# Dealing weight conversions out over the first ups, and moving two checks and a load

## The chip, the cores and the metric

The kernel runs on one core of a Trainium2 chip. The metric is the device time of one execution, in microseconds. A run is compared with runs of the kernel before on the same chip.

A core has five engines with an instruction queue each, which they work through in order: TensorE (PE, matrix products; PEld are its weight loads), VectorE (DVE), ScalarE (ACT), GpSimd (POOL) and SyncE (SP), which here only issues DMAs. Engines wait for each other by semaphores.

## The reference

Two blocks in a row. The first is a gated linear recurrence over 768 steps for 4 batches of 8 heads, with 48 values a head. The second is a dense block over the 3072 tokens, with an activation that is a softmax times its input, and a normalisation:

```python
# q, k, v, alpha: (4, 8, 768, 48), single precision
for t in range(S):
    state = alpha[:, :, t, :, None] * state + np.einsum('bhd,bhe->bhde', k[:, :, t], v[:, :, t])
    y[:, :, t] = np.einsum('bhd,bhde->bhe', q[:, :, t], state)
x = y.transpose(0, 2, 1, 3).reshape(3072, 384)

h = x @ w_in                       # 384 -> 1024
e = np.exp(h - h.max(-1))
solu = h * e / (e.sum(-1) + 1e-09)
ln = (solu - mean(solu)) / np.sqrt(var(solu) + 1e-06) * g_ln
out = ln @ w_out                   # 1024 -> 384
```

`w_in` and `w_out` come in double precision; everything else, the output too, is single precision.

## The kernel before

**Groups.** The sequence is cut into six groups of 128 steps. A group takes that stretch of all four batches at once, so 512 tokens. Each group has an attention part (transposes, running products of alpha, masked scores, the products with the values, the state) and a dense part. The dense part has eight *ups* (`up_mm`, `up_act`), each for 128 of the 1024 inner features and all 512 tokens, and then eight half *downs*, four blocks of 128 tokens with two halves of the features.

**An up** is six matmuls on PE into a bank `h` of PSUM (tag "h", two banks), then on ACT the exponential `e` (L408), on DVE the product `room` = h·e (L409), and on ACT its square `u2` (L412). Up f+2 can start on PE only when `room` of up f has been formed, since that frees the bank. A callback given to `up_act` is put between L409 and L412. In the first group `e` and `u2` lie in four places that are used in turn; PE sums them over features with `array_sums`, once after up 3 and once after up 7.

**Order of the work.** Nothing is reordered: `manual_schedule` keeps each engine's instructions in the order in which the program gives them. So the order in the source is the order in each queue.

**The weights** are fetched in eight pieces (0 to 3 of `w_in`, 4 to 7 of `w_out`) as raw double words into `room`, six slots of 1536 words. Piece 0 goes to slot 3, piece 1 to slot 4, pieces 2 and 3 interleaved to slots 1 and 2, piece 4 to slot 3 again, 5 and 6 to 1 and 2, 7 to 3. A fetch into a slot waits until all that read the slot before have ended. In the first group the products of the ups go to the slots 0, 5 and 4, slot 4 from up 6 on.

Each piece is *converted* on DVE by `bits`, in five instructions over 128 x 768 words: L612, L615 (the upper word's bits moved and its sign put in), L620, L623, L624 (the lower word added). The intermediate values lie in `lots`, a pair for even and a pair for odd pieces. Pieces of `w_out` are then scaled by the gains on ACT (`scaled`, L631).

Each piece is also *checked* on ACT by `in_range`, with a square (L598) and an exponential (L601), each followed by the reading of its sum; the two halves can be issued apart. `alpha_over` is a check of a group's alpha of the same kind (L196, two instructions with two readings). The sums decide at the very end whether a second, general path runs; in these runs it doesn't.

**The first group's ups.** Before them pieces 0 and 1 are converted and checked. Before the change, `bits` of the pieces 2 to 5 is split between the ups, two steps behind an even up and three behind an odd one; pieces 6 and 7 are converted whole behind the last up. The halves of the checks of the pieces 2, 3 and 4 lie in the ups 0 to 5. The pieces 5 to 7 are checked later, in the second group.

**Behind the ups**, in the order of the source: `turned` for the keys of the second group (L164), `load` of the third group's keys, `array_sums`, `down(0, 0)`, `token_sums(0)` (on PE L462, on DVE L467 and three small instructions), `alpha_T(1)` (transposes on DVE, L179 and L182), `down(1, 0)`, `turned` for the queries, then on DVE the scans (L204) and products of the second group, the query products last (L799). On PE stand between them `mean` (L645, L652; it needs all of `w_out`) and more downs. Then PE does the scores of the second group (`scores(1, 0)`, L278); their banks are those from which L799 reads. The rows of the queries that the scores of the state need are moved by DMA (`move_lasts`, `move_firsts`), the state is decayed on GpSimd (`decay`, L261), and PE reads it (`read_state`, L333).

Of the kernel before, what the change touches and what calls it, by code (L numbers as in the profile page):

```python
# [11 lines left out]
U32 = mybir.dt.uint32  # L12
I32 = mybir.dt.int32
AF = mybir.ActivationFunctionType
ALU = mybir.AluOpType
# [17 lines left out]
def fast_path(ctx, tc, q, k, v, alpha, moe_w_in, moe_w_out, moe_g_ln, out):  # L33
# [65 lines left out]
    an = const.tile([P, H, TQ, D], FP, name="an")  # L99
# [31 lines left out]
    def load(src, dst, g):  # L131
        t = slice(g * P, (g + 1) * P)
        for b in range(B):
            nc.sync.dma_start(
                out=dst[32 * b : 32 * b + 32].rearrange("t h u d -> t h (u d)"),
                in_=src[b, :, t, :].rearrange("h (t u) d -> t h (u d)", u=TQ),
            )
# [5 lines left out]
    def load_first(src, dst, g):  # L143
        t = slice(g * P, (g + 1) * P)
        for b in range(0, B, 2):
            nc.sync.dma_start(
                out=by_token(dst)[:, b : b + 2].rearrange("p b h d -> p (b h) d"),
                in_=src[b : b + 2, :, t].rearrange("b h p d -> p (b h) d"),
            )
# [28 lines left out]
    def firsts(src, dst):  # L178
        nc.vector.transpose(out=dst.rearrange("p h (t u) -> p h u t", u=TQ), in_=src[:, :, :, 0:E0])  # L179

    def lasts(src, dst):
        nc.vector.transpose(  # L182
            out=dst.rearrange("p j (i t u) -> p u j i t", u=TQ, i=2),
            in_=src[:, :, :, E0:D].rearrange("p (j i) u d -> p u j i d", i=2),
        )

    def alpha_T(g):
        nc.gpsimd.memset(aT[:, :, 0:1], 0.0)
        firsts(an, aT[:, 0:H, 1:SW])
        lasts(an, aT[:, H:NB, 1:SW])  # L190

    def alpha_over(g):
        x = an.rearrange("p h u d -> p (h u d)")
        sq = one.tile([P, 768], FP, name="sq").bitcast(U8)[:, 0 : x.shape[1]]
        for i, sign in enumerate((1.0, -1.0)):
            nc.scalar.activation(  # L196
                out=sq, in_=x, func=AF.Relu, scale=sign, bias=mone, accum_out=over[:, g, i : i + 1]
            )
# [184 lines left out]
    def u_of(g, f):  # L383
        return slots[((0, 5, 4), (1, 2, 3))[g % 2][f // 3]][:, T4 * (f % 3) : T4 * (f % 3) + T4]
# [5 lines left out]
    def up_mm(g, f):  # L390
        d = gr[g]
        h = ps_h.tile([P, T4], FP, tag="h", name="h")
        for a in range(KC):
            nc.tensor.matmul(  # L394
                h, lhsT=w_in[:, a, f * P : (f + 1) * P], rhs=d["x"][:, a].rearrange("p b t -> p (b t)"),
                start=(a == 0), stop=(a == KC - 1),
            )
        d["h"] = h

    def up_act(g, f, between=None):  # L400
        d = gr[g]
        h = d["h"]
        if g:
            e, u2 = (ring.tile([P, T4], FP, name=x) for x in ("e", "u2"))
        else:
            e, u2 = (sT[:, f % 4, 4 * i : 4 * i + 4].rearrange("p b t -> p (b t)") for i in range(2))
        u = u_of(g, f)
        nc.scalar.activation(out=e, in_=h, func=AF.Exp)  # L408
        nc.vector.tensor_tensor(out=u, in0=h, in1=e, op=ALU.mult)  # L409
        if between:  # L410
            between()
        nc.scalar.activation(out=u2, in_=u, func=AF.Square)  # L412
        d[f] = e, u2
# [16 lines left out]
    def array_sums(g, half):  # L430


        d = gr[g]
        if half == 0:
            d["q"] = [ps_a.tile([P, T4], FP, tag=f"a{i}", name=f"quarters{i}") for i in range(2)]
        for i in range(2):
            for f in range(4):
                r = quarter(f)
                nc.tensor.matmul(
                    d["q"][i][r], lhsT=ones[:, 0:32], rhs=d[4 * half + f][i], start=half == 0, stop=half == 1,  # L440
                    tile_position=(0, r.start), skip_group_check=True,
                )
        if half:
            d["p"] = one.tile([P, 2, T4], FP, name="p")
            for i in range(2):
                nc.scalar.copy(out=d["p"][:, i], in_=d["q"][i])
            d["unit"] = small_ones
# [53 lines left out]
    def down(n, half, part=range(HF)):  # L501
        g, b = divmod(n, B)
        d = st[n]
        if half == 0 and 0 in part:
            d["o"] = ps_o.tile([P, 512], FP, tag="o", name="o")
        for f in (half * HF + i for i in part):
            nc.tensor.matmul(  # L507
                d["o"][:, 0 : DM + 1], lhsT=u_of(g, f)[:, b * P : b * P + P], rhs=w_out[:, f], start=(f == 0),
                stop=(f == FC - 1), skip_group_check=True,
            )  # L510
# [45 lines left out]
    float64 = moe_w_in.dtype != FP  # L556
# [4 lines left out]
    def place(i):  # L561
        kind, f = pieces[i]
        return w_out[:, f : f + 2, 0:DM] if kind else w_in[:, :, f * P : f * P + 2 * P]
# [22 lines left out]
    made = {}  # L586
# [3 lines left out]
    def in_range(i, parts=(0, 1)):  # L590


        if not float64:
            return
        if 0 in parts:
            hi = raws[i][:, :, :, 1].bitcast(FP)
            squares[i] = one.tile([P, F], FP, name="sq").rearrange("p (c f) -> p c f", c=hi.shape[1])
            nc.scalar.activation(out=squares[i], in_=hi, func=AF.Square, accum_out=far[:, i, 0:1])  # L598
        if 1 in parts:
            sq = squares.pop(i)  # L600
            nc.scalar.activation(out=sq, in_=sq, func=AF.Exp, scale=-(2.0**24), accum_out=far[:, i, 1:2])  # L601

    def bits(i, part=None):
        if not float64:
            return
        lo, hi = raws[i][:, :, :, 0], raws[i][:, :, :, 1]
        if part != 1:
            made[i] = [
                lots[2 * (i % 2) + x].rearrange("p (c f) -> p c f", c=hi.shape[1]) for x in range(2)
            ]  # L610
            top = made[i][0].bitcast(U32)
            nc.vector.tensor_scalar(  # L612
                out=top, in0=hi, scalar1=3, scalar2=0x3FFFFFF8, op0=ALU.logical_shift_left, op1=ALU.bitwise_and
            )
            nc.vector.scalar_tensor_tensor(  # L615
                out=top, in0=hi, scalar=0xC0000000, in1=top, op0=ALU.bitwise_and, op1=ALU.bitwise_or
            )
        if part != 0:
            top, low = made.pop(i)
            nc.vector.tensor_scalar(  # L620
                out=low.bitcast(U32), in0=top.bitcast(U32), scalar1=0xFF800000, scalar2=None, op0=ALU.bitwise_and
            )
            nc.vector.scalar_tensor_tensor(out=low, in0=lo, scalar=2.0**-52, in1=low, op0=ALU.mult, op1=ALU.mult)  # L623
            nc.vector.tensor_tensor(out=place(i), in0=low, in1=top, op=ALU.add)  # L624

    def scaled(i):
# [62 lines left out]
    def three(name, where):  # L689
        return [pool.tile([P, NP, P], FP, tag=tag, name=f"{name}{i}") for i, (pool, tag) in enumerate(where)]  # L690
# [13 lines left out]
    for i in range(3):  # L704
        part = slice(NP * i, NP * i + NP)
# [5 lines left out]
    for i in (0, 2, 1):  # L711
        if i == 1:
            scan_on(0, i)
        part = slice(NP * i, NP * i + NP)
        nc.vector.tensor_tensor(
            out=qe[:, :, 0:P] if i == 2 else qv[:, part, 0:P], in0=t[i], in1=aT[:, part, 1:SW], op=ALU.mult
# [13 lines left out]
    keys_back(0)  # L730
    in_range(0)
    bits(1)
    in_range(1)

    for f in range(FC):
        up_mm(0, f)
        if f == 4:
            array_sums(0, 0)
        up_act(0, f, (lambda: in_range(2 + f // 2, (f % 2,))) if f < 6 else None)

        bits(2 + f // 2, f % 2)
        if f == 0:
            next_state(0)
            fetch(4, 3)
            load_first(k, kn, 1)
            load_first(q, qn, 1)
            load(alpha, an, 1)
        elif f == 2:
            ends_k = ends_of(kn, "e")
        elif f == 3:  # L750
            fetch(5, 1)
            fetch(6, 2)
            ends_q = ends_of(qn, "u2")
        elif f == 5:
            fetch(7, 3)
            load_v(1)
        elif f == 6:
            scaled(4)
    bits(6)
    tk = three("tp_k", [(ps_a, "a2"), (ps_a, "a3"), (ps_h, "h")])  # L760
    turned(kn, ends_k, tk)
    load(k, kn, 2)
# [1 line left out]
    scaled(5)  # L764
    down(0, 0)
    scaled(6)
    bits(7)
    token_sums(0)
    alpha_T(1)
    down(1, 0)  # L770
    scaled(7)
    tq = three("tp_q", [(ps_a, "a0"), (ps_a, "a1")])
    turned(qn, ends_q, tq, range(H))
    for i in range(3):
        scan_back(1, i)
        part = slice(NP * i, NP * i + NP)
# [4 lines left out]
    mean(1)  # L781
    down(0, 1, (2, 3))
    hold(0)
    alpha_over(1)
    load(alpha, an, 2)
    tq += three("tp_q2", [(ps_h, "h")])
    turned(qn, ends_q, tq, range(H, NB))
    down(1, 1)
# [7 lines left out]
    for i in range(2):  # L796
        scan_on(1, i)
        part = slice(NP * i, NP * i + NP)
# [165 lines left out]
    def compare(out, x, bound, op):  # L964
# [6 lines left out]
        out=chunks[:, :, 2], in0=sums[:, :, 2], scalar=0.25, in1=sums[:, :, 3], op0=ALU.mult, op1=ALU.is_le  # L971
# [6 lines left out]
    else:  # L978
# [9 lines left out]
        out=bad, in0=all_ok[0:1, 0:1], scalar1=float(P * ends[-1]), scalar2=None, op0=ALU.is_lt  # L988
# [451 lines left out]
```

## Time and profile before

| | |
|---|---|
| median of 3 runs | 373.24 us (372.33 to 374.39) |
| the profiled execution | 374.51 us, of which the span in the profile is 372.6 us |
| mean granted TensorE clock | 0.995 |
| PE busy | 361.1 us, 97% of the span |
| DVE busy | 244.9 us, 66% |
| ACT busy | 147.2 us, 40% |
| POOL busy | 124.6 us, 33% |
| the first group's ups on PE | 28.8 to 53.3 us |
| the second group's ups on PE | from 101.6 us |

Times in the views are microseconds from the start of the span. In a timeline each line has the start, the length, the engine, the line of the kernel, the operation and its tiles; instructions of one kind in a row are merged (x48 stands for 48 of them). In square brackets stands how long the engine was idle before, and what it waited for. A line of windows has the stretch and its length, the busy time and number of instructions of PE, PEld, DVE, ACT and POOL, then PE's granted clock (1.00 is full speed), the share of the DMA engines, and GB/s. Matmuls are pipelined and their ends modelled, so PE's pace is best read from start to start.

### The profile page before, as it was taken

To read this page: it belongs to the slowest core of one execution; us is meant where nothing else is said; L and a number is where in the kernel's file an instruction comes from. 1 tells how busy PE (TensorE), PEld (TensorE's weight loads), DVE (VectorE), ACT (ScalarE), POOL (GpSimd) and SP (SyncE) were. 2 spreads that over 40 slices of the span, in tenths; PEclk is the share of its full clock that TensorE was granted. 3 is DMA by queue.
4 is the path that set the end of the run, shared out by engine and by line. 5 is a ranking of instruction groups with operands and counts; after the bars stand their busy time and mean duration, and the time that the engine had idled before them with its cause. 6 is when DMAs were issued, how large, how long until landed. Compare 5 with 4: busy or idle time off the path is not lost. (4 is left out here: it accounts for less than half of the span.)

```text
span 372.6 us, 10040 instructions
## 1 busy us (share of the span) xinstructions
PE 361.1 (97%) x4341; PEld 215.8 (58%) x4341; DVE 244.9 (66%) x375; ACT 147.2 (40%) x260; POOL 124.6 (33%) x129
## 2 busy tenths in 40 slices
PE   8889999979999999999999999999999999999994
PEld 7775355556755566566575566575555565555552
DVE  1997979978998888945666945666946223544500
ACT  3649853591556262251532251532231231332100
POOL 7020000001367973573114573114582211333200
PEclk9999999998999999999999999999999999999999
DMA  9995986066177608453036253004050000000011
GB/s 181 187 326 144 217 270 139 2 135 152 67 161 165 153 3 168 111 137 84 25 86 145 68 136 86 25 4 106 21 129 9 23 23 0 24 22 21 30 39 49
DMA packets 72871, 36.06 MB, mean 97 GB/s; under 512 B 48232, under 2 KB 70000, under 8 KB 72816
## 3 DMA queue, kind: packets, MB, share of 16 engines
q1 hardware_dynamic: 71792, 34.39, 39.5%
q10 hardware_dynamic: 1024, 0.92, 0.7%
q8 instruction: 36, 0.59, 0.7%
q14 instruction: 19, 0.16, 0.1%
HBM read 25.30 MB, written 4.72 MB: 81 GB/s over the span
## 5 line engine op out<-in xcount | busy, mean ns | idle before, releaser
L507 PE MATMUL o<-w_out,room 128*128 128x385 f32 x384 | 134.8, 495 | 0.0
L394 PE MATMUL h<-x,w_in 128*128 128x512 f32 x288 | 132.2, 599 | 0.6 <-ACT x L363 0.6
L507 PEld LDWEIGHTS o<-w_out,room 128*128 128x128 f32 x384 | 71.6, 191 | 55.3 <-issue 14.7
L394 PEld LDWEIGHTS h<-x,w_in 128*128 128x128 f32 x288 | 52.7, 189 | 58.3 <-issue 48.4
L409 DVE TENSOR_TENSOR room<-h,e 128x512 f32<-128x512 f32 x40 | 27.6, 690 | 60.0 <-ACT e L408 60.0
L408 ACT ACTIVATE e<-h 128x512 f32<-128x512 f32 x40 | 23.9, 597 | 93.8 <-PE h L394 93.6
L427 POOL TENSOR_TENSOR p<-p,e 128x512 f32<-128x512 f32 x30 | 42.5, 1416 | 27.3 <-ACT e L408 27.0
L412 ACT ACTIVATE u<-room 128x512 f32<-128x512 f32 x40 | 25.2, 630 | 38.2 <-DVE room L409 38.2
L546 POOL TENSOR_TENSOR r<-sums,mhalf 128x1 f32<-128x1 f32 x20 | 12.8, 639 | 77.3 <-DVE sums L537 77.1
L289 DVE TENSOR_TENSOR sT<-a,mask 128x512 f32<-128x512 f32 x43 | 26.7, 683 | 14.4 <-PE a L278 14.4
L427 DVE TENSOR_TENSOR p<-p,u 128x512 f32<-128x512 f32 x30 | 24.4, 814 | 7.2 <-ACT u L412 7.2
L204 DVE TENSOR_TENSOR_SCAN hT<-aT,unit 128x516 f32<-128x516 f32 x18 | 23.4, 1342 | 7.6 <-ACT aT L697 7.5
L204 DVE TENSOR_TENSOR_SCAN aT<-aT,seed 128x516 f32<-128x516 f32 x18 | 27.9, 1578 | 0.2
L278 PEld LDWEIGHTS a<-qv,kT 32*128 32x128 f32 x704 | 21.9, 189 | 8.8 <-DVE qv L799 2.7
L278 PE MATMUL a<-qv,kT 32*128 32x128 f32 x704 | 24.6, 282 | 2.1 <-DVE qv L799 1.9
L333 PE MATMUL y<-sT,vn 128*32 128x128 f32 x768 | 22.9, 274 | 1.0 <-issue 0.8
L212 POOL COPY fend<-hT 128x12 f32<-128x12 f32 x6 | 4.1, 676 | 59.0 <-DVE hT L204 59.0
L333 PEld LDWEIGHTS y<-sT,vn 128*32 128x32 f32 x768 | 20.8, 110 | 4.4 <-issue 3.8
L225 POOL TENSOR_TENSOR kT<-kT,hT 128x1024 f32<-128x1024 f32 (+1 forms) x8 | 14.2, 1805 | 21.1 <-DVE kT L179 21.1
L196 ACT ACTIVATE sq<-an,mone 128x1536 uint8<-128x1536 f32 x12 | 18.9, 1575 | 0.2
L548 ACT ACTIVATE o_sb<-o,r 128x384 f32<-128x384 f32 x16 | 9.3, 581 | 24.1 <-POOL r L546 24.1
L363 ACT COPY x<-y 128x384 f32<-128x384 f32 x24 | 11.2, 479 | 7.3 <-PE y L333 7.1
(148 smaller groups left out, 364.5 us busy)
## 6 DMA issues: line engine op xcount, KB each, us to landing
vn<-in_v_dram SPq DMA_DIRECT2D x24, 192.0 KB, 4.4
an<-in_alpha_dram SPq DMA_DIRECT2D x20, 192.0 KB, 4.2
out_dram<-o_sb SPq DMA_DIRECT2D x20, 192.0 KB, 1.9
room<-in_moe_w_out_dram SPq DMA_DIRECT2D x8, 384.0 KB, 4.8
kn<-in_k_dram SPq DMA_DIRECT2D x16, 192.0 KB, 4.2
qn<-in_q_dram SPq DMA_DIRECT2D x16, 192.0 KB, 3.9
lot<-qe SPq DMA_DIRECT2D x40, 64.5 KB, 2.1
lot<-qv SPq DMA_DIRECT2D x20, 129.0 KB, 2.4
```

The lines of the kernel that those rows point to most:

```text
L196: nc.scalar.activation(out=sq, in_=x, func=AF.Relu, scale=sign, bias=mone, accum_out=over[:, g, i : i + 1])
L204: nc.vector.tensor_tensor_scan(out=o, data0=a, data1=s, initial=1.0, op0=ALU.mult, op1=ALU.add)
L225: nc.gpsimd.tensor_tensor(out=kT[:, part], in0=kT[:, part], in1=hk[:, part], op=ALU.mult)
L278: nc.tensor.matmul(a[b][:, i], lhsT=kT[quarter(b), kb], rhs=qv[quarter(b), qb, 0:P], start=not last and not i, stop=bool(last), tile_posit ...
L289: nc.vector.tensor_tensor(out=sT[:, b, half * NP : half * NP + NP], in0=a[b], in1=mask[:, None, :].to_broadcast([P, NP, P]), op=ALU.mult,)
L333: nc.tensor.matmul(y_bank(b)[quarter(r), a], lhsT=lhsT, rhs=rhs, start=(b, r) not in begun, stop=stop, tile_position=(row, 32 * r), skip_g ...
L394: nc.tensor.matmul(h, lhsT=w_in[:, a, f * P : (f + 1) * P], rhs=d["x"][:, a].rearrange("p b t -> p (b t)"), start=(a == 0), stop=(a == KC ...
L408: nc.scalar.activation(out=e, in_=h, func=AF.Exp)
L409: nc.vector.tensor_tensor(out=u, in0=h, in1=e, op=ALU.mult)
L412: nc.scalar.activation(out=u2, in_=u, func=AF.Square)
L427: eng.tensor_tensor(out=p, in0=d[0][i] if f == 1 else p, in1=d[f][i], op=ALU.add)
L507: nc.tensor.matmul(d["o"][:, 0 : DM + 1], lhsT=u_of(g, f)[:, b * P : b * P + P], rhs=w_out[:, f], start=(f == 0), stop=(f == FC - 1), skip ...
```

## The change

It regroups where work of the first group is issued; no instruction is added or left out, apart from the order. `bits` is split into single steps (`bit(i, k)`, k from 0 to 4).

- The steps of the pieces 2 to 7 form one list, and the ups 0 to 7 take 4, 2, 3, 3, 3, 3, 3 and 9 steps of it. Behind the ups no step is left.
- The second piece's check (piece 1) goes from ahead of up 0 into up 4. Piece 4's check, half in up 4 and half in up 5 before, lies whole in up 5. The checks of the pieces 2 and 3 stay.
- The second group's alpha check, `alpha_over(1)`, goes from behind `hold(0)` to behind `scaled(6)`, where the conversion of piece 7 stood. The load of the third group's alpha, `load(alpha, an, 2)`, goes from there to behind `alpha_T(1)`.

```diff
-    def bits(i, part=None):
-        if not float64:
-            return
+    def bits(i, steps=range(5)):
+        for k in steps if float64 else ():
+            bit(i, k)
+
+    def bit(i, k):
         lo, hi = raws[i][:, :, :, 0], raws[i][:, :, :, 1]
...
     bits(1)
-    in_range(1)
+
+    steps = [(i, step) for i in range(2, 8) for step in range(5)]
+    checks = {0: [(2, 0)], 1: [(2, 1)], 2: [(3, 0)], 3: [(3, 1)], 4: [(1, 0), (1, 1)], 5: [(4, 0), (4, 1)]}
+
+    def check(f):
+        for i, part in checks.get(f, ()):
+            in_range(i, (part,))
 
     for f in range(FC):
         up_mm(0, f)
         if f == 4:
             array_sums(0, 0)
-        up_act(0, f, (lambda: in_range(2 + f // 2, (f % 2,))) if f < 6 else None)
-
-        bits(2 + f // 2, f % 2)
+        up_act(0, f, lambda: check(f))
+        for _ in range((4, 2, 3, 3, 3, 3, 3, 9)[f]):
+            step = steps.pop(0)
+            if float64:
+                bit(*step)
...
-    bits(6)
     tk = three("tp_k", [(ps_a, "a2"), (ps_a, "a3"), (ps_h, "h")])
     turned(kn, ends_k, tk)
     load(k, kn, 2)
...
     scaled(6)
-    bits(7)
+    alpha_over(1)
     token_sums(0)
     alpha_T(1)
+    load(alpha, an, 2)
     down(1, 0)
...
     hold(0)
-    alpha_over(1)
-    load(alpha, an, 2)
```

More of the change, by code (lines that the diff above doesn't have):

```diff
@@ L601, in in_range @@
             nc.scalar.activation(out=sq, in_=sq, func=AF.Exp, scale=-(2.0**24), accum_out=far[:, i, 1:2])
-    def bits(i, part=None):
-        if not float64:
-            return
+    def bits(i, steps=range(5)):
+        for k in steps if float64 else ():
+            bit(i, k)
+    def bit(i, k):
         lo, hi = raws[i][:, :, :, 0], raws[i][:, :, :, 1]
-        if part != 1:
+        if k == 0:
             made[i] = [
@@ L610, in bits @@
             ]
-            top = made[i][0].bitcast(U32)
+        top, low = made[i]
+        bits_top = top.bitcast(U32)
+        if k == 0:
             nc.vector.tensor_scalar(
-                out=top, in0=hi, scalar1=3, scalar2=0x3FFFFFF8, op0=ALU.logical_shift_left, op1=ALU.bitwise_and
+                out=bits_top, in0=hi, scalar1=3, scalar2=0x3FFFFFF8, op0=ALU.logical_shift_left, op1=ALU.bitwise_and
             )
+        elif k == 1:
             nc.vector.scalar_tensor_tensor(
-                out=top, in0=hi, scalar=0xC0000000, in1=top, op0=ALU.bitwise_and, op1=ALU.bitwise_or
+                out=bits_top, in0=hi, scalar=0xC0000000, in1=bits_top, op0=ALU.bitwise_and, op1=ALU.bitwise_or
             )
-        if part != 0:
-            top, low = made.pop(i)
+        elif k == 2:
             nc.vector.tensor_scalar(
-                out=low.bitcast(U32), in0=top.bitcast(U32), scalar1=0xFF800000, scalar2=None, op0=ALU.bitwise_and
+                out=low.bitcast(U32), in0=bits_top, scalar1=0xFF800000, scalar2=None, op0=ALU.bitwise_and
             )
+        elif k == 3:
             nc.vector.scalar_tensor_tensor(out=low, in0=lo, scalar=2.0**-52, in1=low, op0=ALU.mult, op1=ALU.mult)
+        else:
             nc.vector.tensor_tensor(out=place(i), in0=low, in1=top, op=ALU.add)
```

## The prediction

> **What bounds the kernel now.** I read the page first. TensorE (PE) is busy for 97% of the span and no other engine for more than 66%, so time can only come from PE's holes or from a slow PE. The chain that ended last has only three pieces and tells nothing about the middle. So I went to the waits of PE: three holes behind the load phase are named for VectorE (DVE), all between 66 and 82 us. The timeline of PE places them, the half-microsecond windows show PE's clock, and the timelines of DVE, ScalarE (ACT) and the DMA queue (SP) say why DVE is late.
>
> From the timeline of PE (start, length, what, in brackets the idle time before and who ended it):
>
> ```profile
> 53.28 1.95 PE L164 MATMUL tp_k<-ident,kn 128*32 128x128 f32 x64
> ...
> 66.46 1.63 PE L645 MATMUL sums<-w_out,ones 128*32 128x384 f32 x16 [0.57 <-DVE cols L467]
> ...
> 79.77 0.48 PE L278 MATMUL a<-qv,kT 32*128 32x128 f32 x2 [0.54 <-DVE qv L799]
> 81.64 2.64 PE L278 MATMUL a<-qv,kT 32*128 32x128 f32 x62 [1.38 <-DVE qv L799]
> 84.21 3.91 PE L507 MATMUL o<-w_out,room 128*128 128x385 f32 x8
> 88.05 2.07 PE L278 MATMUL a<-qv,kT 32*128 32x128 f32 x64
> 90.04 2.86 PE L507 MATMUL o<-w_out,room 128*128 128x385 f32 x8
> 92.83 1.16 PE L333 MATMUL y<-lot,state 64*32 64x128 f32 x64
> ```
>
> Before 53.28 the ups run without a hole: PE sets their pace (48 matmuls, about 0.443 us from start to start). Then there are three holes, 2.5 us together, and a block that is slow without a hole: eight down matmuls take 3.91 us at 84.21 and 2.86 at 90.04. The windows (PE's granted clock is the last column but two) say why:
>
> ```profile
> 82.00:82.50 0.50, 0.50 (x28) 0.50 (x24) 0.00 (x0) 0.47 (x3) 0.00 (x0) 1.00 0.47 106
> 83.00:83.50 0.50, 0.50 (x20) 0.50 (x15) 0.00 (x0) 0.47 (x2) 0.00 (x0) 0.50 0.50 128
> 86.00:86.50 0.50, 0.50 (x2) 0.20 (x1) 0.50 (x2) 0.00 (x0) 0.00 (x0) 0.64 0.76 165
> 86.50:87.00 0.50, 0.50 (x3) 0.23 (x3) 0.50 (x1) 0.00 (x0) 0.00 (x0) 1.00 1.19 248
> ```
>
> The clock is 0.50 from about 82.9 to 86.2, just behind the two holes, and 1.00 in every other window that I read from 28 to 106 us. So the holes are paid twice.
>
> DVE, from the end of the prologue's conversions to the last query product (L409 is `room` = h·e of an up, L612 to L624 the five conversion steps, L467 the row sums, L799 the query products):
>
> ```profile
> 34.27 0.69 DVE L409 TENSOR_TENSOR room<-h,sT 128x512 f32<-128x512 f32 x1 [1.88 <-ACT sT L408]
> ...
> 48.87 0.69 DVE L409 TENSOR_TENSOR room<-h,sT 128x512 f32<-128x512 f32 x1 [1.22 <-ACT sT L408]
> ...
> 54.81 0.69 DVE L409 TENSOR_TENSOR room<-h,sT 128x512 f32<-128x512 f32 x1 [0.74 <-ACT sT L408]
> ...
> 65.09 0.96 DVE L624 TENSOR_TENSOR w_out<-lot 128x768 f32<-128x768 f32 x1
> 65.97 0.44 DVE L467 STREAM_TRANSPOSE cols<-rows 128x256 f32<-128x256 f32 x1
> ...
> 80.89 0.69 DVE L799 TENSOR_TENSOR qv<-tp_q,aT 128x512 f32<-128x512 f32 x1
> ```
>
> From 65.97 to 81.58 DVE doesn't pause. What delays it are the conversions ahead of 65.97, and among them it idles three times, each time for the exponential of an up. The first is late because ACT does a check first:
>
> ```profile
> 31.72 0.97 ACT L598 ACTIVATE sq<-room 128x768 f32<-128x768 f32 x1
> ...
> 33.66 0.58 ACT L408 ACTIVATE sT<-h 128x512 f32<-128x512 f32 x1
> ...
> 71.94 1.58 ACT L196 ACTIVATE sq<-an,mone 128x1536 uint8<-128x1536 f32 x1
> ```
>
> **The change, part by part.**
>
> *The second piece's check* (four ACT instructions, 31.72 to 33.66) leaves the place ahead of the first exponential. Up 0 is done on PE at 31.55, so that exponential can start at about 31.7 and `room` 0 at 32.30, when the second piece's conversion is through (31.43 + 0.87): 1.97 us sooner, and DVE's 1.88 us hole is gone. The check reappears in up 4. There ACT now has half a check (1.0 us) and then idles 1.33 us up to 48.24; the full check takes 1.97, so it eats 1.0 of that hole and the exponential of up 5, which waits for PE, doesn't move. Cost nothing; without the hole it would be 1 us on ACT.
>
> *The conversion steps dealt out* (4, 2, 3, 3, 3, 3, 3, 9 for ups 0 to 7, against 2 and 3 in turn and ten behind the ups). No step is added or dropped, so DVE's work between 32.30 and the row sums stays 65.97 − 32.30 − 3.84 (the three holes) = 29.8 us; only the idle time changes. I walked it with the pitches of the trace: `room` 0.60, steps 0.58 (0.98 for the pieces 2 and 3), 0.99, 0.58, 1.00, 0.88. `room` 0 to 7 come out at 32.3, 36.4, 39.0, 42.1, 45.3, 48.9, 51.9, 54.9 (before: 34.3, 36.9, 40.0, 42.5, 45.5, 48.9, 51.9, 54.8). New idle time: 0.2 in ups 1 and 2, 0.3 in up 4 (the exponential of up 4 stands behind the copy of `qn`, whose DMA ends the wait at 44.16), 0.5 in up 5 (PE), 0.3 in up 6. That is about 1.1 to 1.3 us instead of 3.84, so the row sums start at about 63.2 instead of 65.97: DVE is 2.75 us earlier. No up is hurt: up f+2 needs the bank that `room` f frees, and up 3 starts at 38.29 where `room` 1 ends at 37.0, up 4 at 40.95 where `room` 2 ends at 39.6, up 7 at 50.7 where `room` 5 ends at 49.5. The margins are 1.2 us or more; before, the smallest was 0.25.
>
> *Piece 4's check*, both halves now in up 5, holds ACT from 48.7 to 50.7; the square of up 5 and the exponential of up 6 queue behind it, and the latter starts at 51.25 instead of 50.81. That is the 0.3 us on DVE above. The fetch of piece 7 waits for the check's first half (49.8) instead of the conversion's fourth step (51.02); with 4.1 us to land it is there at 54, and wanted at 59. Piece 5 is the tight one: wanted at 49.5 instead of 52.5. Its two transfers were issued at 44.7 and 45.1 and landed 3.6 and 4.8 us later, 49.9 at the last. Its slot is free at 42.1 now and SP at 42.85, but the DMA engines were full at 1.1 in that stretch, so I give it no more than half a microsecond: a wait of 0 to 0.4, most of which falls into the 0.3 of idle time in up 6.
>
> *The alpha check* (four instructions, 71.94 to 75.31, 3.37 us) goes ahead of the gains of piece 7. ACT waits there now, 2.52 and 2.92 us for `w_out`. In the new order piece 6 is converted at 59.0 and scaled to 60.6, the check runs to 63.9, piece 7 (converted at 63.1) is scaled to 65.0. The sums over `w_out` need it at 67.1 at the earliest, so 2 us of cover; beyond that each microsecond would be one on PE.
>
> *Alpha's third load* (four DMAs on SP, 75.34 to 77.13) waits for the transposes of the second alpha, which end at 67.2 now, and issues up to 69. Behind it on SP stand the eight moves of the queries' last rows; their data come at 75.1 instead of 77.85, so SP is free for them, where the old place would have held them for 2 us. The state's decay on GpSimd, which ends at 89.48, follows the moves and comes 2.75 us earlier, at 86.7; the first read of the state is due at 88.4, so 1.6 us of cover.
>
> *On PE.* The hole of 0.57 goes: the row sums are read at 63.7, PE comes at 65.9. Everything up to the second down moves by 0.57, and PE is ready for the scores at about 78.5 (its last down matmul starts at 78.75 and the pitch is 0.33). The second query product ends at 81.58 − 2.75 = 78.85, so a hole of 0.3 to 0.4 remains of 1.9. The scores resume at 78.89 instead of 81.64: 2.75 us. Then the clock: 62 score and 8 down matmuls took 81.64 to 88.05, 6.41 us; undisturbed, 64 take 1.99 (88.05 to 90.04) and 8 take 2.79 (90.04 to 92.83), so 1.93 + 2.79 = 4.72, and 1.69 more is won if the clock stays up. I take that it does: the hole of 0.57 at 66 is the nearest row, and the clock was 1.00 behind it. The bounds of this term are 0 and 1.69.
>
> The Trainium skill speaks against the clock term: "TensorE: Matmul & The Clock Gate" (Part 1, and the section on HAM oscillation) has the clock halve after a whole idle window of about 3.4 us. By that rule holes of 0.5 and 1.4 us would not have lowered it, and only the holes would be won, 2.75; the trace shows half clock for about 3.4 us behind them, so I go by the trace.
>
> Sum: 2.75 + 1.69 = 4.44 us. Behind 93 us PE has one hole, 0.60 us at 136.95, and the next DVE chain (the third group's scans) moves by 4.2, with 1.1 us of cover before up 2 of the second group; so it stays won. The profiled execution took 374.51 us (span 372.6), so 370.1 for such a one; that is 1.27 above the median of the runs, 373.24, so 368.8, said as 368.9.
>
> **Rivals.**
> 1. *Half of it.* Piece 5 lands 1 to 2 us later than reckoned, or ACT is slower between its checks; DVE comes 1 to 1.5 us earlier, a hole of 1.3 to 1.8 stays ahead of the scores and the clock may fall as now. Gain 1 to 3.2, so 370.0 to 372.2. For it: the DMA engines are full from 37 to 49 us. Against it: 0.3 us of idle time behind it absorbs the first part.
> 2. *Too little to tell.* The gain is partly given back by a transfer. If the queries' moves land no earlier than now, the decay ends at 89.5, PE waits 1.1 us for it at 88.4, and a clock window could be lost there, 1.69: 4.44 − 2.79 = 1.65 us, so 371.6. Against it: the moves wait for DVE's data, and SP is idle before them.
> 3. *Slower.* The four steps of up 0 outrun their cover. They fit only because the first exponential starts at 31.7. If it starts after 33.6 all the same (ACT's first check and the copies ahead of it running late), `room` 1 ends at 39.0 against 38.29 and `room` 2 follows late too: 0.7 to 1.4 us of holes among the ups, a clock window of 1.7, and the DVE chain no earlier than now. Price 2 to 3 us: 375 to 376. It decides from a start of about 33.0 on. Against it: nothing but up 0 and the first piece's check stands before that exponential.
>
> That the steps are empty (weights given in single precision) is out: the L612 to L624 rows are there.
>
> **How the numbers follow.** About 0.5% (1.9 us) can be told from no change here. The sum, 4.44 with ends at 2.75 (clock not won) and 4.8 (no hole left ahead of the scores), gets 0.80; rival 1 0.11; rival 2 0.05; rival 3 0.04. Half of rival 1 lies above the 0.5% line of 371.4 us. So faster 0.87, same 0.09, slower 0.04. The range, 367.9 to 371.4, takes in the sum's two ends, the spread of the runs and half of rival 1.
>
> **What would show it.** Right: the first L409 at 32.3, no hole over 0.6 us on DVE among the ups, L467 at about 63, the last L799 ending near 78.9, the eight down matmuls behind the first scores in 2.9 us, clock 1.00 throughout. Wrong: a hole ahead of an L394 matmul, a wait of L612 for a DMA in up 5 over 0.5 us, L467 later than 64.5, a clock of 0.50 anywhere behind 10 us, or PE waiting for the state's decay near 88.

## The result and the profile after

The changed kernel takes 370.12 us (median of 4 runs, 369.71 to 370.72) against 373.55 (4 runs, 372.33 to 374.39); the ratio is 0.9908 with an interval of 0.9879 to 0.9937. It is faster by 3.43 us, and the time lies in the range, 1.2 us above the value said. The profiled execution took 370.72 us, span 368.9; against the profiled one of before, 374.51, that is 3.79.

The timeline of PE after, the rows that answer to the three holes and the slow downs:

```profile
65.64 1.48 PE L651 MATMUL sums<-w_out,ones 128*32 128x384 f32 x16
...
78.18 2.41 PE L278 MATMUL a<-qv,kT 32*128 32x128 f32 x64
80.52 2.86 PE L507 MATMUL o<-w_out,room 128*128 128x385 f32 x8
83.31 2.07 PE L278 MATMUL a<-qv,kT 32*128 32x128 f32 x64
85.30 2.86 PE L507 MATMUL o<-w_out,room 128*128 128x385 f32 x8
88.09 1.16 PE L333 MATMUL y<-lot,state 64*32 64x128 f32 x64
```

No row has an idle time in brackets any more. The first scores take 2.41 us where the second take 2.07: the 0.34 us left of the hole lie inside them. The eight downs take 2.86. The half-microsecond windows show PE's clock (last column but two) full where it was 0.50 and 0.64:

```profile
83.00:83.50 0.50, 0.50 (x6) 0.20 (x8) 0.50 (x1) 0.50 (x2) 0.00 (x0) 1.00 0.87 190
86.00:86.50 0.50, 0.50 (x3) 0.31 (x2) 0.50 (x2) 0.00 (x0) 0.47 (x2) 1.00 1.04 219
```

The timeline of DVE (the conversion is at L616 to L630 now, the query products at L811):

```profile
32.29 0.68 DVE L409 TENSOR_TENSOR room<-h,sT 128x512 f32<-128x512 f32 x1
...
48.80 0.69 DVE L409 TENSOR_TENSOR room<-h,sT 128x512 f32<-128x512 f32 x1 [0.51 <-ACT sT L408]
...
61.84 0.96 DVE L630 TENSOR_TENSOR w_out<-lot 128x768 f32<-128x768 f32 x1
62.72 0.44 DVE L467 STREAM_TRANSPOSE cols<-rows 128x256 f32<-128x256 f32 x1
...
77.78 0.69 DVE L811 TENSOR_TENSOR qv<-tp_q,aT 128x512 f32<-128x512 f32 x1
```

Of three waits (3.84 us) one is left, 0.51, and a small one of 0.16 at 39. The row sums start 3.25 us sooner and the query products end at 78.47 instead of 81.58. On PE the second group's first up comes at 96.80 instead of 101.62, so 4.82 sooner, but the end is only 3.7 sooner. The rest goes mostly in the second group's ups, to two waits that the profile of before doesn't have (timeline of PE, after):

```profile
113.14 2.27 PE L278 MATMUL a<-qv,kT 32*128 32x128 f32 x64 [0.30 <-POOL qv L253]
...
124.05 1.01 PE L333 MATMUL y<-lot,state 64*32 64x128 f32 x48 [0.57 <-POOL state L261]
```

Two questions were left for the chip: what each part of the change earns, and how much of the gain is the clock.

### The profile page after: what moved, and what is told of

Its sections match the earlier page's. It is cut to its first block, busy times and chain, and to the rows that moved or that the text cites. A ratio compares the mean times of both kernels' runs of the same rounds, so it can differ in the third digit from the quotient of the medians.

```text
span 368.9 us, 10039 instructions
## 1 busy us (share of the span) xinstructions
PE 359.6 (97%) x4341; PEld 215.7 (58%) x4341; DVE 244.8 (66%) x375; ACT 146.6 (40%) x260; POOL 124.4 (34%) x129
## 5 line engine op out<-in xcount | busy, mean ns | idle before, releaser
L427 POOL TENSOR_TENSOR p<-p,e 128x512 f32<-128x512 f32 x30 | 41.5, 1383 | 26.7 <-ACT e L408 26.4
L278 PE MATMUL a<-qv,kT 32*128 32x128 f32 x704 | 23.8, 279 | 0.3 <-POOL qv L253 0.3
```

The costliest lines, as they stand in the source:

```text
L278: nc.tensor.matmul(a[b][:, i], lhsT=kT[quarter(b), kb], rhs=qv[quarter(b), qb, 0:P], start=not last and not i, stop=bool(last), tile_posit ...
L427: eng.tensor_tensor(out=p, in0=d[0][i] if f == 1 else p, in1=d[f][i], op=ALU.add)
```

## The experiments

Each time stands beside that of the kernel before, measured together with it. Those medians are 373.86, 374.17 and 373.96. They depend on how many of the executions are of a slower kind (9 of 22, 11 of 17, 5 of 13; see the experiments on the clock), and so do the ratios. The quicker executions alone have a median of 372.89, 372.89 and 373.13.

**The changed kernel once more** (`after_again`, no edit).

> The changed kernel once more, with a second profile. In the first one PE is 4.82 us ahead at the second group's first up (96.80 against 101.62) and 3.79 ahead from the second read of the state on. Theory A (the third group's chain of query products, moves and state decay has no cover left): the wait for the state on PE comes back, 0.5 to 0.9 us, and PE is 3.6 to 4.0 ahead behind it. Theory B (an accident of that execution, the third move of the queries' first rows having taken 2.34 us to issue on SP): the wait is gone, PE stays 4.5 ahead, and the time is about 0.8 below the first profiled execution (370.72), so 369.9.

370.28 us against 373.86, ratio 0.9916 (0.9886 to 0.9946). The profiled execution took 370.06. PE in it:

```profile
112.95 2.27 PE L278 MATMUL a<-qv,kT 32*128 32x128 f32 x64
...
122.83 1.26 PE L333 MATMUL y<-lot,state 64*32 64x128 f32 x64
```

Neither wait is there. Counted from the start of up 0, PE is 4.56 ahead of the first profile of before at the second read of the state (94.23 against 98.79) and 4.26 at its last matmul. So the 1.03 us given back in the first profile belong to that execution (theory B; 369.9 was said), but the cover is thin. The two state products, on POOL:

```profile
121.38 1.64 POOL L261 TENSOR_TENSOR state<-state,lot 128x384 f32<-128x384 f32 x2 [0.80 <-DMA lot<-qv]
```

They end at 123.02, 0.19 after PE has begun to read. One of the four moves of the first rows that they wait for held SP for 2.10 us here, 2.34 in the first profile after and 1.53 in the first before, the other three 0.6 each. The waits don't need the change: a second profile of before (`before_again`) had the one for the state too, 0.70 us, and two more of before (`before_look2`, `before_look3`) the one for the queries, 0.28 us each. What makes that move long stays open.

**The hole filled** (`filled`).

```diff
     down(2, 0)
+    warm(8)
     scores(1, 0)
```

> The kernel before with eight dummy products (16 matmuls of 128 columns, about 2.2 us) on PE ahead of the second group's scores, so that the hole from 79.1 to 81.6 us is busy and nothing else changes; the scores start at 81.64 as before. If the half clock comes of the hole, as the prediction has it: clock 1.00 from 82 to 87, eight down matmuls in 2.9 us instead of 3.9, and 1.2 to 1.7 us won: 371.9 to 372.4 against 373.6. If the clock is lowered for another reason (the small matmuls of the scores, or a fixed window): clock 0.50 as before, 373.6 or later.

The timeline of PE:

```profile
79.09 1.95 PE L452 MATMUL warm<-ones 128*128 128x128 f32 x16
...
81.66 2.06 PE L278 MATMUL a<-qv,kT 32*128 32x128 f32 x62 [0.21 <-DVE qv L799]
83.65 2.86 PE L507 MATMUL o<-w_out,room 128*128 128x385 f32 x8
```

The scores resume where they did (81.64), the downs take 2.86, the clock is 1.00, and the second group's first up comes at 99.94 instead of 101.62: 1.68 us, the clock term alone (1.69 said). But the median fell by 0.65 only, 373.21 against 373.86, ratio 0.9987 (0.9968 to 1.0006), half of the 1.2 to 1.7 expected. The single executions say why. The experiments together have 64 of the kernel before, and they fall into two groups (called heaps below): 31 have a mean clock of 0.992 to 0.995 and a median of 374.44 us, 33 have 0.997 to 1.000 and a median of 372.89. With the hole filled all ten have 0.997 or more and lie between 372.7 and 373.9. Their median, 373.21, is 1.4 us below that of the nine slower ones measured together with them (374.59) and 0.3 above that of the thirteen quicker ones (372.89). So filling wins about 1.4 us in the slower executions and nothing in the others.

**The kernel before, to see the others** (`before_again`, `before_look2`, `before_look3`, no edit).

> The kernel before, with a profile of its own. Its 22 executions so far fall into two heaps: nine with a mean clock of 0.992 to 0.995 take 374.2 to 374.9 us, thirteen with 0.998 to 1.000 take 372.5 to 374.1, their median 372.9. Theory A (the half clock behind the holes depends on where a window that runs freely falls): both heaps come again, about two in five in the slower one, 1.6 to 1.8 us apart; where the profile is of the quicker heap, the two holes ahead of the scores are there (0.5 and 1.4 us), the clock is 1.00 behind them and the eight down matmuls take 2.9 us. Theory B (in the quicker executions DVE comes sooner): the holes are shorter there by 1 us or more, with L799 ending that much earlier.

374.19 against 374.17, ratio 0.9994 (0.9974 to 1.0013): six of ten at a clock of 0.994 or 0.995, four above. So the share of the slower heap isn't fixed: with the 17 beside them it is 17 of 27 here, where two in five were expected. The profile was of the lower clock; two more executions were profiled.

> The kernel before once more, for a profile of its quicker heap. Theory A (the window's phase decides): if the mean clock is 0.998 or more, the holes of 0.5 and 1.4 us ahead of the scores are there all the same, the clock is 1.00 behind them, eight down matmuls take 2.9 us, and the second group's first up comes 1.7 us sooner after up 0 than in the first profile (71.1 instead of 72.8). Theory B (a quicker DVE): shorter holes. If it falls into the slower heap: as in the first profile.

> As the other look at the kernel before: in a profile of the quicker heap the same two holes with a clock of 1.00 behind them (theory A), or shorter holes (theory B).

They took 373.04 and 373.01 us with clocks of 0.999 and 0.998. PE in the first of them:

```profile
79.49 0.48 PE L278 MATMUL a<-qv,kT 32*128 32x128 f32 x2 [0.53 <-DVE qv L799]
81.35 2.06 PE L278 MATMUL a<-qv,kT 32*128 32x128 f32 x62 [1.38 <-DVE qv L799]
83.34 2.86 PE L507 MATMUL o<-w_out,room 128*128 128x385 f32 x8
```

The holes are the same, 0.53 and 1.38, and the clock stays at 1.00 in every window from 75 to 90 us. So theory B is out: DVE is no quicker; the same holes lower the clock in one execution and not in the next. That a free-running window decides, as theory A says, can be read from when the clock changes. Three half-microsecond windows, the first two of `before_again`, the third of `before_look2` (at the end, when PE is done, the clock falls again):

```profile
85.50:86.00 0.50, 0.50 (x2) 0.34 (x3) 0.50 (x2) 0.00 (x0) 0.00 (x0) 0.70 0.60 127
372.50:373.00 0.50, 0.00 (x0) 0.00 (x0) 0.00 (x0) 0.00 (x0) 0.00 (x0) 0.52 0.06 16
...
370.00:370.50 0.50, 0.00 (x0) 0.00 (x0) 0.00 (x0) 0.00 (x0) 0.00 (x0) 0.67 0.04 16
```

A mean of 0.70 puts the return to full clock at 85.80, one of 0.52 the fall at the end at 372.52: 286.72 us apart, which is 84 times 3.413. And the half clock lasts 3.41 us in all three profiles of this place that have it (from 82.94 in the first one of before, 82.39 in `before_again`, 81.86 in `check_only` below). So the clock changes only at the ends of periods of 3.41 us, and where these periods lie against the holes differs from one execution to the next.

In these three profiles the period just before the half clock holds 1.6, 1.9 and 1.9 us of PE's idle time. In `before_look2` the fall at the end is at 370.17; 85 periods earlier is 80.04, which is between the two holes but for 0.07 us, so one period holds 0.6 us of idle time and the next 1.3. In `before_look3` the fall at the end is at 369.98, and the same counting gives 79.85, with 0.5 and 1.4. In this place, then, the clock fell behind a period with 1.6 us of idle time or more and stayed behind one with 1.4 or less. Idle time alone isn't the whole rule: in `split_moves` below a period with 1.7 us of it, from 121.5 on, left the clock at 1.00.

**Half of the hole filled** (`half_filled`: `warm(4)` in place of `warm(8)`).

> The kernel before with four dummy products (8 matmuls, about 1.1 us) ahead of the scores: the hole ahead of them shrinks from 2.5 us of no issue to about 1.3. If half of the hole is still enough for the half clock in some phases, two heaps remain, 1.7 us apart, the slower one rarer than before (below two in five); if it isn't, all executions have a clock of 0.997 or more and lie between 372.5 and 373.9, as with the hole filled.

373.18 against 373.96, ratio 0.9986 (0.9963 to 1.0008), with the second hole at 1.11 us and the downs at 2.86. All ten clocks are 0.997 or more; with 5 slower ones in the 13 beside them, the chance of that would be about one in 130 if nothing had changed. Two of the ten lie at 374.1, outside the span expected, at full clock; their cause wasn't profiled. No period of 3.41 us can hold more than the 1.1 us of idle time that are left ahead of the scores, which is below the 1.4 that left the clock alone in `before_look3`.

**The second piece's check put back** (`check_back`).

```diff
     bits(1)
+    in_range(1)
...
-    checks = {0: [(2, 0)], 1: [(2, 1)], 2: [(3, 0)], 3: [(3, 1)], 4: [(1, 0), (1, 1)], 5: [(4, 0), (4, 1)]}
+    checks = {0: [(2, 0)], 1: [(2, 1)], 2: [(3, 0)], 3: [(3, 1)], 5: [(4, 0), (4, 1)]}
```

> The changed kernel with the second piece's check put back ahead of up 0; the steps stay dealt out 4, 2, 3, ... Theory (the deal needs the early exponential): L409 of up 0 at 34.2, of up 1 at 38.4, a hole of 0.7 us on PE ahead of up 3, the row sums 1.9 us later at 64.6, a hole of 1.5 us ahead of the scores; 1.9 us lost if the clock stays up, 3.6 if it falls, less up to 0.8 that is no longer given back: 371.4 to 373.7. Rival (the deal alone earns the gain, the check's place matters nothing): no hole among the ups, 370.1 to 370.5.

370.53, ratio 0.9924 (0.9897 to 0.9951): the rival. In the timeline of DVE:

```profile
33.24 0.69 DVE L409 TENSOR_TENSOR room<-h,sT 128x512 f32<-128x512 f32 x1 [0.78 <-ACT sT L408]
37.29 0.68 DVE L409 TENSOR_TENSOR room<-h,sT 128x512 f32<-128x512 f32 x1
...
48.74 0.69 DVE L409 TENSOR_TENSOR room<-h,sT 128x512 f32<-128x512 f32 x1
...
62.67 0.44 DVE L467 STREAM_TRANSPOSE cols<-rows 128x256 f32<-128x256 f32 x1
```

The first product is 0.95 us later than in the changed kernel, and in up 5 DVE has caught up: the 0.51 us that it waits there in the changed kernel, and the small waits before it, are its reserve. The row sums come at 62.67. The time is 0.25 us above the changed kernel's beside it (370.28). In this execution ACT was done with the prologue's copies 1 us sooner than in the profiles that the expectation was worked out from, so the first exponential came at 32.64 and not at 33.6.

**The deal alone** (`deal_only`: the kernel before with the steps dealt out 4, 2, 3, 3, 3, 3, 3, 9; all checks and the load where they were).

> The kernel before with the conversions dealt out (4, 2, 3, 3, 3, 3, 3, 9) and nothing else: the second piece's check ahead of up 0, piece 4's check in two halves, the alpha check and alpha's load behind the hold. Theory (the deal alone is the gain, as the run with the check put back says): row sums at 62.7 to 63.2, no hole ahead of the scores, 370.2 to 370.9. Rival (the moves carry part of it): the load holds the moves of the queries up to 76.2 instead of 74.8, PE waits for the state near 88; 371 to 372.5.

371.10 against 374.17, ratio 0.9925 (0.9899 to 0.9951): most of the gain. Against the quicker executions of before it is 1.8 us, where the changed kernel (370.28) wins 2.6. The time lies just outside what the theory said, at the edge of its rival's range. ACT was done with the prologue's copies at 29.4, 0.7 us later than in `check_back`, and the first exponential came at 33.38; the timelines of DVE and PE show what the prediction's slower rival said:

```profile
38.05 0.69 DVE L409 TENSOR_TENSOR room<-h,sT 128x512 f32<-128x512 f32 x1
```

```profile
38.78 5.42 PE L394 MATMUL h<-x,w_in 128*128 128x512 f32 x12 [0.67 <-DVE room L409]
```

Up 3 waits 0.67 us for `room` of up 1. It costs no clock, and 0.26 of it is made good at the scores, which then find their queries ready and take 2.15 us instead of 2.41. So in these two profiles the check's old place costs PE 0 and 0.7 us, by how late ACT leaves the prologue. The rival's own sign is small: the moves of the queries start at 76.96, the state's decay ends at 88.84 where PE reads from 88.54, and that read takes 1.37 us instead of 1.16.

**The checks alone** (`check_only`: the kernel before with only the two weight checks moved).

> The kernel before with only the checks moved: the second piece's into up 4, piece 4's whole into up 5. Conversions as before, two and three in turn and ten steps behind the ups. Theory (early exponential and deal only pay together): the hole of 1.88 us at 34 is gone but comes back as waits for later exponentials (1.5 us ahead of up 1, 1.4 ahead of up 5), row sums at about 65.7, PE holes and half clock as before: 373.0 to 373.6. Rival (the check alone is the gain): row sums at 64.1, the hole ahead of the scores below 0.3, 370.5 to 371.7.

374.23 against 373.86, ratio 1.0003 (0.9979 to 1.0027): nothing, as the theory said. The median is above the span expected because six of the ten are of the slower heap; the medians of its two heaps, 374.44 and 372.97, are like those of before beside it (374.59 and 372.89).

```profile
36.45 0.69 DVE L409 TENSOR_TENSOR room<-h,sT 128x512 f32<-128x512 f32 x1 [1.25 <-ACT sT L408]
...
48.80 0.69 DVE L409 TENSOR_TENSOR room<-h,sT 128x512 f32<-128x512 f32 x1 [1.50 <-ACT sT L408]
...
65.91 0.44 DVE L467 STREAM_TRANSPOSE cols<-rows 128x256 f32<-128x256 f32 x1
```

The hole ahead of up 0 is gone and stands ahead of ups 1 and 5: with two steps to an up DVE runs out of work until PE has the next one.

**The alpha check and load put back** (`alpha_back`).

```diff
     scaled(6)
-    alpha_over(1)
     token_sums(0)
     alpha_T(1)
-    load(alpha, an, 2)
...
     hold(0)
+    alpha_over(1)
+    load(alpha, an, 2)
```

> The changed kernel with the second alpha's check and the third alpha's load at their old place behind the hold. SP issues the load from 74.4 to 76.2 and the moves of the last rows 1.4 us later than in the changed kernel; the state's decay ends at 87.8 instead of 86.4, PE comes at 88.1. Theory (covered): 370.0 to 370.6, no wait for the state at 88. Rival (cover too thin): a wait of 0.5 to 1.5 us there, 370.8 to 372.

370.86 against 374.17, ratio 0.9912 (0.9885 to 0.9938). The ratio is like the changed kernel's 0.9916, but more of the executions beside it were of the slower heap; in time it is 0.6 us above the changed kernel's 370.28, with four executions from 369.82 to 371.12, and so above what the theory said. The state is ready in time (POOL, ends at 87.37; PE reads from 87.86), so the cover holds as expected. But PE has another hole:

```profile
92.37 0.38 PE L333 MATMUL y<-lot,state 64*32 64x128 f32 x2 [0.78 <-issue]
```

`deal_only`, with the load at the old place too, has it at the same matmul (0.93), the changed kernel in neither profile. The bracket says `issue`: PE waits for nothing that the profile shows. A like one (0.5 to 0.8) stands in the prologue of several profiles. PE comes to the second group's first up at 98.08 instead of 96.80. Whether the load's place has to do with the hole, and with the 0.6 us, stays open.

**Half of the moves on ACT** (`split_moves`), a try at a better version: the third group's moves of the last query rows for odd heads issued by ACT behind up 4.

```diff
-            move_lasts()
+            move_lasts((0,) if a == 2 else range(2))
+        elif what == "rest":
+            move_lasts((1,), nc.scalar)
```

> The changed kernel with half of the third group's moves of the last query rows issued by ACT in up 4 instead of by SP, so that SP is free for the first rows 2.4 us sooner. Theory (what is given back in the second group hangs on SP's row of twelve moves): the decay at L261 starts without a wait for its DMA, right behind POOL's sums at about 120.7, no PE wait for the state, the profile ahead by 4.4 to 4.6 of the kernel before at the third group's ups, 369.6 to 370.1. Rival (ACT's four issues, 2.4 us, hold back the exponential of up 5, or POOL is the bound itself): no gain, 370.2 to 371.2.

377.51 against 374.17, ratio 1.0096 (1.0076 to 1.0117): slower, and for neither reason. The waits of SP's queue and the timeline of PE:

```profile
SPq L176 <- DMA lot<-qe: 7.8, 1, 7.8
```

```profile
128.13 2.43 PE L333 MATMUL y<-lot,state 64*32 64x128 f32 x64 [4.90 <-POOL state L261]
```

The last load of the values, which SP issues ahead of its own moves, now waits 7.8 us, by the profile for one of the moves (`lot<-qe`), which ACT issues only at 116.0, so all of SP's moves come late. Why a load waits for a move that it doesn't need isn't shown. The run shows the price of a late state: 4.9 us of hole, and a clock of 0.50 from 128.3 to 131.7 behind it.

## Why the prediction was right, and where it wasn't

**DVE's order: right.** `room` was worked out for 32.3, 36.4, 39.0, 42.1, 45.3, 48.9, 51.9 and 54.9 and came at 32.3, 36.4, 39.0, 42.1, 45.2, 48.8, 51.7 and 54.6. The row sums came at 62.72 (63.2 said), the query products ended at 78.47 (78.85 said), and 0.34 us of the hole were left (0.3 to 0.4 said). Piece 5 made nobody wait: DVE's first step of it ran at 49.40 straight behind `room` 5. PE was 4.82 us ahead at the second group's first up, where 4.44 was said.

**Where the 1.88 us went: half right.** The prediction gave the first wait to the check's move. `check_only` and `deal_only` show that the move alone earns nothing and the deal alone most of the gain: with enough steps behind each product DVE doesn't run dry, whichever wait stood there. The move guards against the prologue's spread. The slower rival's mechanism was real, and so was its mark of about 33.0 for the first exponential (no hole from 32.64, one from 33.38), but the hole was 0.67 us and the price not 2 to 3.

**The clock term: right in mechanism, too large for a median.** It is 1.68 us where it occurs, but it occurs in 31 of 64 executions of the kernel before. The prediction went by one profiled execution, which was one of these, and carried its 4.44 us over to the median; so the time came out 1.2 us above the 368.9 said. Against the slower executions the sum holds: 374.59 to 370.28 is 4.31. Against those at full clock only the holes are won: 372.89 to 370.28 is 2.61, by the prediction's term 2.75. With the clock term taken at 31/64 of the 1.55 us between the two medians, 0.75, the sum is 3.5 us, and 3.43 was measured, 3.58 in `after_again`. The prediction gave the profiled execution's distance from the median, 1.27 us, no cause; it was one of the slower ones.

The Trainium skill, "TensorE: Matmul & The Clock Gate" (Part 1), lets the window of about 3.4 us run freely. The runs agree with that part: the clock changes at the ends of periods of 3.41 us, and the same holes fall into one period or into two. They don't agree that the window must be wholly idle, since a period with 1.6 us of idle time was enough.

**"So it stays won": too quick.** The prediction looked for later waits in the second group's state only. The third group's had little cover before the change: POOL's products ended 0.35 us ahead of PE in the first profile of before, and PE waited 0.70 for them in `before_again`. With PE 4.8 sooner and DVE 4.5 the wait came in one of two profiles, 0.57 us, with 0.30 before it for the queries; the median of the changed kernel isn't told apart by it (370.12 and 370.28).

**The alpha edits: the cover held, a gain isn't shown.** In the changed kernel neither edit made PE wait. The 2 us that the old place would have held SP were 1.2 in `alpha_back` (moves at 76.05 instead of 74.81), and the state was still 0.5 us early there. Whether the 0.6 us between the two kernels' times come of the old place stays open.

## What to carry to other kernels

Where one engine in order does both what others wait for and bulk work that nobody waits for yet, deal the bulk out so that each wait has enough of it behind it; moving a wait alone only moves the idle time to the next one. Two holes on PE of 1.9 us together cost 1.5 us more in half of the executions here: look at the clock of all runs before a profiled one's loss is carried over to the median. And after a stage has been won, check the cover of the same step one stage on, too.

## What the runs showed of the hardware that was not expected

- The same two holes of PE (0.5 and 1.4 us, behind an earlier one of 0.6) went with a lower mean clock in 31 of 64 executions, 1.55 us between the medians; in the slower ones that were profiled the clock was 0.50 for 3.41 us. With 8 dummy matmuls in the hole (1.11 us idle left) it was so in none of 10. The clock changes at the ends of periods of 3.41 us, and the fall came where one period held 1.6 us or more of the holes.
- With four transfers issued from ACT's queue instead of SP's, a load on SP waited 7.8 us, by the profile for one of these transfers, though the kernel has the load first; why isn't shown.
- In the third group's row of four moves on SP one takes 1.3 to 2.3 us to issue and the others 0.6, in eight of eight profiles.
